# One product for the local scores of two heads: k laid block-diagonally in a fused attention and expert kernel

## The chip, the cores and the metric

The kernel runs on one core of a Trainium2 chip. A core has a matrix engine (TensorE, PE in the profile; its weight loads are listed apart as PEld), VectorE (DVE), ScalarE (ACT), GpSimd (POOL) and a queue that issues transfers (SyncE, SP). Each engine works through its own list of instructions in order and waits on semaphores for the others. [...]

The metric is the device time of one execution in microseconds; lower is better.

## The reference

For 8 batches of 8 heads with 576 positions of 64 numbers, two attentions are added: one over positions averaged by fours (144 of them), repeated four times, and a local one, in which a position sees only the positions less than 4 away.

```python
q_d = q.reshape(B, H, Sd, factor, D).mean(axis=3)          # k_d, v_d alike
out_up = np.repeat(sm_attn(q_d, k_d, v_d), factor, axis=2)
mask = np.abs(pos[:, None] - pos[None, :]) < factor        # factor = 4
scores = scale * np.matmul(q, k.transpose(0, 1, 3, 2))     # scale = 1 / 8
scores = np.where(mask, scores, -1000000000.0)
...                                                        # softmax over the last axis
out_local = np.matmul(attn, v)
return out_up + out_local
```

The sum, with the heads side by side as 4608 tokens of 512 numbers, goes through a mixture of 8 experts: each token is sent to one expert (the largest logit, with a bias by modality), `out = gate * (relu(x @ w1) @ w2)`.

## The kernel before

The attention runs in 32 **steps**, one for two heads; four steps make a batch. The two heads lie above each other in the 128 partitions, head 0 in partitions 0 to 63 and head 1 in 64 to 127. A step n does this:

- `tpq`, `tpk`, `tpt`: TensorE transposes 512 of the 576 positions of q and k (tiles qt and kt, loaded by SP) to PSUM; `tpt`, in every second step, does the remaining 64 of two steps.
- `qT`, `kT_`: ScalarE copies these out of PSUM, to `qT2` and `kT2`. With i = 0 the main 128x512, with i = 1 (every second step) the rest, 128x128. Each has room for two steps, by `n % 2`.
- `mk`, `sc`: the local scores. 576 positions are cut into 24 strips of 24 positions, and a strip sees a window of 32 positions of k. `mk` puts the mask into PSUM with a product, and `sc` adds to it 24 products of 64x24 by 64x32, one for each strip, for one head. Four strips lie in the four quarters of the 128 output partitions. Each 32-bit product shows as two records in the trace. `mk0` and `sc0` do head 0, `mk1` and `sc1` head 1.
- `lm`, `le` (VectorE), `exp` (ScalarE), `z`, `zr` (VectorE), `nl` (GpSimd, a product of tile le with zr), `lt` (VectorE, a transpose), `Pw_` (ScalarE): the softmax of the local scores, and the layout in which `avl` (TensorE) multiplies it with v (tile vw).
- `qe`, `qd`, `d`, `kd`: GpSimd adds q and k by fours, in two sums each; `halves` adds pairs at a distance of two (qe, d), `whole` the rest. `scd`, `dm`, `de`, `nd`, `pdt`, `PdT`, `avd`, `Od` are the averaged attention: scores (TensorE), maximum (VectorE), exponential (ScalarE, tile de), normalization (`nd`, GpSimd, tile de), transposes (`pdt`, TensorE), copies (ScalarE), product with the averaged v (`vp`, `vc` make tile vd), scaling.
- `X`: VectorE adds the two outputs.

Names in the trace are those of tiles: `nl` is GpSimd's instruction on tile le at L391, `nd` that on tile de at L395. The router of a finished batch (`lg` to `st`, `R`, `store`) runs beside the steps of the next: products with the gate, some 20 small VectorE instructions, four or five scatters of table entries by GpSimd (tab), transposes of X (R) and their stores. Behind the attention come the experts: loads of weights, their split into two parts, and products of 512 columns.

The order of work on each engine in the attention is written out by hand: every piece has a time in steps in the table `PHASE` (a piece of step n is issued at n + its time, `kT0` at 0.2050, `sc0` at 0.5591, `zr` at 2.2907 for n two steps earlier), and all pieces are issued in the order of these times. PSUM buffers are shared: tag S (3 buffers) by `mk`/`sc` and `scd`, tag T (3) by the transposes and `vp`, tag A (2) by `avd`, `avl` and the router's products. The functions that the change touches, and their callers:

Of the kernel before, what the change touches and what calls it, by code (L numbers as in the profile page):

```python
# [7 lines left out]
F32 = mybir.dt.float32  # L8
F32R = mybir.dt.float32r
BF16 = mybir.dt.bfloat16  # L10
I32 = mybir.dt.int32
AF = mybir.ActivationFunctionType
ALU = mybir.AluOpType
# [4 lines left out]
B, H, S, D = 8, 8, 576, 64  # L18
# [4 lines left out]
SUB, WIN = 24, 32  # L23
BLK = 4 * SUB
NB = 6
PAD = 3
KT = S - SUB + WIN
QS = 1.0 / 128
NEG = -8.0e9 * QS
# [17 lines left out]
TB, SB = 3, 3  # L47
# [30 lines left out]
class Consts:  # L78
    def __init__(s, tc, pool, psum):
        nc = tc.nc  # L80

        s.ps = psum
        pool.tile([128, 48], F32, name="pad")
        s.dummy = pool.tile([128, 128], BF16, name="dummy")
        nc.vector.memset(s.dummy, 0.0)
        s.busy(nc, 12)
        s.ident = pool.tile([128, 128], F32, name="ident")
        make_identity(nc, s.ident)
        s.identb = pool.tile([128, 128], BF16, name="identb")
        make_identity(nc, s.identb)  # L90

        x = pool.tile([128, 1], F32, name="warm")
        nc.vector.memset(x, 0.0)
        nc.scalar.activation(x, x, AF.Exp)
        m = pool.tile([128, WIN], BF16, name="band")
        nc.gpsimd.memset(m, 0.0)
        for j in range(4):
            t = m[32 * j : 32 * j + 32]
            nc.gpsimd.affine_select(out=t, in_=t, pattern=[[1, WIN]], compare_op=ALU.is_ge, fill=NEG, base=0,
                                    channel_multiplier=-1)  # L100
            nc.gpsimd.affine_select(out=t, in_=t, pattern=[[-1, WIN]], compare_op=ALU.is_ge, fill=NEG, base=6,
                                    channel_multiplier=1)
        s.mask = pool.tile([128, NB, WIN], BF16, name="mask")
        nc.vector.tensor_copy(s.mask, m.unsqueeze(1).broadcast_to([128, NB, WIN]))
        nc.vector.memset(s.mask[0:32, 0, 0:PAD], NEG)
        nc.vector.memset(s.mask[96:128, NB - 1, SUB + PAD : WIN], NEG)

        s.pool = pool.tile([128, 32], F32, name="pool")

# [18 lines left out]
    def load(s, tc, pool, work, rows, mid, bias, w_gate):  # L128
        nc = tc.nc
        s.wg = pool.tile([128, 4, 32], F32, name="wg")  # L130
        nc.vector.memset(s.wg, 0.0)
        for f in range(2):
            for a in range(2):
                nc.sync.dma_start(s.wg[64 * a : 64 * a + 64, 2 * f : 2 * f + 2, 0:NE],
                                  w_gate[256 * f + 128 * a : 256 * f + 128 * a + 128].rearrange("(g d) e -> d g e", g=2))
        s.mi = rows.tile([128, 2 * DM], F32, name="R", bufs=NR)[:36, :256].bitcast(I32)
        nc.sync.dma_start(s.mi, mid.bitcast(I32).rearrange("(t x) -> t x", t=36))
        s.bb = work.tile([128, 2, NE], F32, name="bb")
        nc.sync.dma_start(s.bb, bias.unsqueeze(0).broadcast_to([128, 2, NE]))
# [53 lines left out]
class Attention:  # L193


    def __init__(s, tc, ctx, ectx, C, psum, q, k, v):
        s.tc, s.C, s.ps = tc, C, psum
        nc = s.nc = tc.nc
        s.q, s.k, s.v = q, k, v

        s.ld = ectx.enter_context(tc.tile_pool(name="ald", bufs=2, side="right", reuse_waits="tile"))
        s.wk = ctx.enter_context(tc.tile_pool(name="awk", bufs=2, reuse_waits="tile"))
        s.one = ctx.enter_context(tc.tile_pool(name="aone", bufs=1, reuse_waits="tile"))
        s.QK, s.t = {}, {}
        s.vw = [(s.ld, s.one)[j].tile([128, H * NB, D], F32, name=f"vw{j}", bufs=1) for j in range(2)]

        s.qT2 = s.ld.tile([128, 2, S], F32, name="qT", bufs=1)
        s.kT2 = s.ld.tile([128, 2, KT], F32, name="kT", bufs=1)
        nc.vector.memset(s.kT2[:, :, 0:PAD], 0.0)
        nc.vector.memset(s.kT2[:, :, S + PAD :], 0.0)  # L210
        s.Pw = [s.one.tile([128, 2 * NB, 4, SUB], F32, name=f"Pw{j}") for j in range(NPW)]

        s.De = [s.one.tile([128, 3, 32 * NB], F32, name=f"de{j}") for j in range(3)]
        for j in range(2):
            nc.vector.memset(s.vw[j][0:32, 0], 0.0)
            nc.vector.memset(s.vw[j][96:128, H * NB - 1], 0.0)

        for j in range(3):
            nc.vector.memset(s.De[j], 0.0)
# [49 lines left out]
    def tp(s, n, nm):  # L269

        src = s.QK[n // 2]["qk".index(nm)]
        p = s.t["tp", nm, n] = s.ps.tile([128, 512], F32, name="tp", tag="T", bufs=TB)
        for j in range(4):
            s.nc.tensor.transpose(p[:, 128 * j : 128 * j + 128],
                                  src[:, 5 * (n % 2) + j].rearrange("p a d -> p (a d)"), s.C.ident)
# [7 lines left out]
    def tpt(s, n, i):  # L283

        p = s.t["tp", "t"] = s.ps.tile([128, 2, 128], F32, name="tpt", tag="T", bufs=TB)
        for x in range(2):
            s.nc.tensor.transpose(p[:, x], s.QK[n // 2][x][:, 4].rearrange("p a d -> p (a d)"), s.C.ident)
# [7 lines left out]

    def kT_(s, n, i):
        g = n % 2
        if i:
            t = s.kT2.rearrange("m g t -> m (g t)")[:, PAD + 512 : PAD + 512 + 2 * (KT - 512)]
            s.nc.scalar.copy(t.rearrange("m (g t) -> m g t", g=2)[:, :, :64], s.t["tp", "t"][:, 1].rearrange("m (g t) -> m g t", g=2))  # L300
        else:
            s.nc.scalar.copy(s.kT2[:, g, PAD + 64 * g : PAD + 64 * g + 512], s.t.pop(("tp", "k", n)))

    def halves(s, nm, n, T):

        d2 = s.t[nm, n] = s.ld.tile([128, 144, 2], F32, name=nm, bufs=1)
        T4 = T.rearrange("m (g t) -> m g t", t=4)
        s.nc.gpsimd.tensor_tensor(d2, T4[:, :, 0:2], T4[:, :, 2:4], op=ALU.add)

    def whole(s, nm, n, d2):  # L310
        dd = s.t[nm, n] = s.ld.tile([128, 144], F32, name=nm)
        s.nc.gpsimd.tensor_tensor(dd, d2[:, :, 0], d2[:, :, 1], op=ALU.add)

    def qe(s, n, i):
        s.halves("qe", n, s.qT2[:, n % 2])

    def qd(s, n, i):
        s.whole("qd", n, s.t.pop(("qe", n)))

    def d(s, n, i):  # L320
        s.halves("d", n, s.kT2[:, n % 2, PAD : PAD + S])

    def kd(s, n, i):
        s.whole("kd", n, s.t.pop(("d", n)))

    def mk(s, n, a):
        p = s.t["sc", n, a] = s.ps.tile([128, NB, WIN], F32, name="sc", tag="S", bufs=SB)
        s.nc.tensor.matmul(p, s.C.identb, s.C.mask, start=True, stop=False, skip_group_check=True)

    def sc(s, n, a):  # L330

        p, qT, kT = s.t["sc", n, a], s.qT2[:, n % 2], s.kT2[:, n % 2]
        r = slice(64 * a, 64 * a + 64)
        for i in range(NB):
            for j in range(4):
                q0 = BLK * i + SUB * j
                s.nc.tensor.matmul(p[32 * j : 32 * j + SUB, i, :], qT[r, q0 : q0 + SUB], kT[r, q0 : q0 + WIN],  # L337
                                   start=False, stop=(i == NB - 1), skip_group_check=True,
                                   tile_position=(64 * a, 32 * j))

    def lm(s, n, a):
        if ("lm", n) not in s.t:
# [91 lines left out]
    def avl(s, n, i):  # L434

        b, hp = divmod(n, 4)
        vw, Pw = s.vw[b % 2], s.Pw[n % NPW]
        p = s.t["avl", n, i] = s.ps.tile([128, 3, BLK], F32, name="avl", tag="A", bufs=2)
        for c in range(3):
            for a in range(2):  # L440
                k = 3 * i + c
                s.nc.tensor.matmul(p[64 * a : 64 * a + 64, c], vw[:, NB * (4 * (hp // 2) + hp % 2 + 2 * a) + k, :],
                                   Pw[:, NB * a + k], start=True, stop=True, skip_group_check=True)

    def X(s, n, i, dst):

# [782 lines left out]
```

## Time and profile before

| | |
|---|---|
| median of 3 runs | 709.7 us (709.04 to 718.24) |
| profiled execution | 716.96 us, span of its instructions 715.3 us |
| busy in the span | PE 662.0, PEld 535.7, DVE 379.2, ACT 358.7, POOL 262.9 us |
| TensorE's mean granted clock | 0.974 |
| moved | 107.93 MB, 151 GB/s on the mean |
| local scores (sc) | 7.5 to 257.5 us, 3072 records |

Times in the profile count from the first instruction. A timeline row has the start, the time until the last of its instructions ends, the engine, the line, the operation with its tiles and shapes, and how many instructions it merges; in brackets, idle time of the engine just before it and what ended that. A row of groups has the total busy time, the mean of one in ns, and the idle time before them. A row of stretches has the busy time of PE, PEld, DVE, ACT and POOL in that stretch, each with its number of instructions, then the granted clock, the DMA engines' share and GB/s. Ends of products are modelled, and products overlap, so the distance from one start to the next says more than a duration.

### The profile page before, as it was taken

How to read it: one execution, taken by the hardware profiler on the slowest of the kernel's cores; microseconds unless marked ns; L12 is line 12 of the kernel's file. 1: busy time of each engine (PE TensorE's matmuls, PEld its weight loads, DVE VectorE, ACT ScalarE, POOL GpSimd, SP SyncE). 2: the span in 40 equal slices, each digit the busy share in tenths (PEclk: the TensorE clock that was granted, in tenths of full speed). 3: DMA queues.
4: the chain of work that ended last, by engine and by line, in shares of the span. 5: the costliest groups of instructions: out<-in, count | busy, mean ns of one | idle time of the engine just before them, and what ended most of it. 6: DMA issues, size and time to landing. Idle time of an engine off the chain costs nothing. (4 is left out here: it accounts for less than half of the span.)

```text
span 715.3 us, 19216 instructions
## 1 busy us (share of the span) xinstructions
PE 662.0 (93%) x7467; PEld 535.7 (75%) x7467; DVE 379.2 (53%) x877; ACT 358.7 (50%) x804; POOL 262.9 (37%) x351
## 2 busy tenths in 40 slices
PE   7889999998968798999999999999999999999991
PEld 4677776776746666887888888888888888889790
DVE  3678687787848686836533245333453243525510
ACT  3678777777756574534444234433444234444610
POOL 6756665857647857353030310403103011010200
PEclk9799999999989899999999999999999999999996
DMA  9799799897889757579560744516435154346400
GB/s 178 148 186 173 162 165 181 174 184 130 145 147 214 152 151 186 154 228 294 143 219 21 189 148 116 179 58 190 165 102 156 67 162 148 103 133 186 159 13 29
DMA packets 179439, 107.93 MB, mean 151 GB/s; under 512 B 139309, under 2 KB 157777, under 8 KB 179346
## 3 DMA queue, kind: packets, MB, share of 16 engines
q1 hardware_dynamic: 172274, 87.49, 53.1%
q0 software_dynamic: 7072, 19.18, 8.3%
q8 instruction: 60, 0.98, 0.7%
q14 instruction: 33, 0.27, 0.2%
HBM read 87.39 MB, written 19.51 MB: 149 GB/s over the span
## 5 line engine op out<-in xcount | busy, mean ns | idle before, releaser
L938 POOL DMA_INDIRECT out_dram<-o,tg x37 | 40.9, 1106 | 302.7 <-ACT o L937 245.5
L817 DVE TENSOR_TENSOR wlo<-raw,whi 128x1024 fp32r<-128x1024 f32 x73 | 87.4, 1222 | 84.4 <-ACT whi L811 74.4
L891 DVE SCALAR_TENSOR_TENSOR hl<-l,hh 128x512 fp32r<-128x512 f32 x72 | 49.4, 688 | 101.7 <-ACT hh L890 101.7
L934 PE MATMUL l<-whi,hh 128*128 128x512 f32 x256 | 100.2, 395 | 0.0
L934 PE MATMUL l<-wlo,hh 128*128 128x512 f32 x256 | 99.6, 390 | 0.0
L934 PE MATMUL l<-whi,hl 128*128 128x512 f32 x256 | 99.6, 390 | 0.0
L890 ACT ACTIVATE hh<-l 128x512 fp32r<-128x512 f32 x72 | 42.9, 597 | 110.7 <-PE l L886 109.3
L886 PE MATMUL l<-xh,whi 128*128 128x512 f32 (+1 forms) x256 | 95.0, 374 | 0.4 <-DVE hl L891 0.2
L886 PE MATMUL l<-xh,wlo 128*128 128x512 f32 (+1 forms) x256 | 94.8, 370 | 0.0
L886 PE MATMUL l<-xl,whi 128*128 128x512 f32 (+1 forms) x256 | 94.7, 370 | 0.0
L811 ACT CAST whi<-raw 128x1024 fp32r<-128x1024 f32 x70 | 71.4, 1050 | 28.2 <-DMA raw<-in_moe_w_dram 18.2
L937 ACT ACTIVATE o<-l,tg 128x512 f32<-128x512 f32 x37 | 25.3, 687 | 98.5 <-PE l L934 70.5
L407 ACT COPY Pw<-lt 32x288 f32<-32x288 f32 x128 | 54.6, 426 | 3.2 <-DVE lt L402 1.8
L934 PEld LDWEIGHTS l<-wlo,hh 128*128 128x128 f32 x256 | 48.1, 188 | 10.1
L886 PEld LDWEIGHTS l<-xh,whi 128*128 128x128 f32 x256 | 48.1, 188 | 9.7 <-POOL xg L1063 0.5
L934 PEld LDWEIGHTS l<-whi,hl 128*128 128x128 f32 x256 | 48.1, 188 | 9.5
L934 PEld LDWEIGHTS l<-whi,hh 128*128 128x128 f32 x256 | 48.1, 188 | 9.5
L886 PEld LDWEIGHTS l<-xh,wlo 128*128 128x128 f32 x256 | 48.3, 189 | 8.3
L886 PEld LDWEIGHTS l<-xl,whi 128*128 128x128 f32 x256 | 48.3, 189 | 8.0
L337 PE MATMUL sc<-kT,qT 64*24 64x32 f32 x3072 | 45.5, 195 | 8.1 <-issue 7.4
L391 POOL TENSOR_TENSOR le<-le,zr 128x384 f32<-128x384 f32 x32 | 26.8, 836 | 70.0 <-DVE zr L387 53.5
L337 PEld LDWEIGHTS sc<-kT,qT 64*24 64x24 f32 x3072 | 35.3, 101 | 22.8 <-issue 18.2
(241 smaller groups left out, 1277.9 us busy)
## 6 DMA issues: line engine op xcount, KB each, us to landing
raw<-in_moe_w_dram SPq DMA_DIRECT2D x176, 128.0 KB
raw<-in_moe_w_dram SPq DMA_DIRECT2D x44, 512.0 KB
vw<-in_v_dram SPq DMA_DIRECT2D x53, 192.0 KB
qt<-in_q_dram SPq DMA_DIRECT2D x30, 288.0 KB
kt<-in_k_dram SPq DMA_DIRECT2D x30, 288.0 KB
xs<-R SPq DMA_DIRECT2D x64, 128.0 KB
vw<-in_v_dram SPq DMA_DIRECT2D x15, 96.0 KB
xs<-R SPq DMA_DIRECT2D x12, 64.0 KB
```

The lines of the kernel that those rows point to most:

```text
L337: s.nc.tensor.matmul(p[32 * j : 32 * j + SUB, i, :], qT[r, q0 : q0 + SUB], kT[r, q0 : q0 + WIN], start=False, stop=(i == NB - 1), skip_gro ...
L391: s.nc.gpsimd.tensor_tensor(e, e, z[:, : 2 * NB].unsqueeze(2).broadcast_to([128, 2 * NB, WIN]), op=ALU.mult)
L407: s.nc.scalar.copy(s.Pw[n % NPW][r, :, j, :SUB], s.t["lt", n][r, :, :SUB])
L811: (nc.gpsimd.tensor_copy if turn <= 4 else nc.scalar.copy)(hi, raw)
L817: (nc.gpsimd if turn == 4 else nc.vector).tensor_tensor(lo, raw, hi.bitcast(F32), op=ALU.subtract)
L886: nc.tensor.matmul(p[:, f % n, :], a[:, fs], x[:, k, :N], start=(k == 0 and i == 0), stop=(k == 3 and i == 2))
L890: nc.scalar.activation(hh[:, g, :N], p, AF.Relu)
L891: nc.vector.scalar_tensor_tensor(hl[:, g, :N], p, 0.0, hh[:, g, :N].bitcast(F32), op0=ALU.max, op1=ALU.subtract)
L934: nc.tensor.matmul(p, a[:, f, hs], x[:, f % 2, :], start=(f == 0 and i == 0), stop=(f == 7 and i == 2))
L937: nc.scalar.mul(o, p, T[:, h, 1:2].bitcast(F32))
L938: nc.gpsimd.indirect_dma_start(out=s.out[:, :], out_offset=bass.IndirectOffsetOnAxis(ap=T[:, h, 0:1], axis=0), in_=o, in_offset=None, boun ...
```

## The change

`kT2` becomes `kB`, twice as wide: for each of the two steps that it holds there are two rows of positions, one for each head, and head a's k lies in partitions 64a to 64a + 63 of row a; the rest is cleared once and stays zero. A product over all 128 partitions with a strip of q (both heads above each other) and the same window of both rows gives 64 columns: the scores of head 0 and of head 1 beside each other. `sc` now goes by halves of the positions (x = 0, 1) with both heads, 12 products of 128x24 by 128x64 in each call, where it went by heads with 24. The copies of k out of PSUM split by head: of the main part ScalarE copies 64x512 and VectorE the other 64x512; of the rest ScalarE makes four copies of 64x64. The half sums of k (`d`) become two instructions of 64 partitions. The mask needs two forms, since the first and the last strip now lie in different calls, and `avl` reads the weights in the new order of blocks.

```diff
-        nc.vector.memset(s.mask[0:32, 0, 0:PAD], NEG)
-        nc.vector.memset(s.mask[96:128, NB - 1, SUB + PAD : WIN], NEG)
+        nc.vector.memset(s.mask[0:32, 0:2, 0:PAD], NEG)
+        s.band = m
...
-        s.kT2 = s.ld.tile([128, 2, KT], F32, name="kT", bufs=1)
-        nc.vector.memset(s.kT2[:, :, 0:PAD], 0.0)
-        nc.vector.memset(s.kT2[:, :, S + PAD :], 0.0)
+        s.kB = s.ld.tile([128, 2, 2, KT], F32, name="kT", bufs=1)
+        nc.vector.memset(s.kB, 0.0)
+        s.mask = s.one.tile([128, NB, WIN], BF16, name="mask")
+        nc.vector.tensor_copy(s.mask, C.band.unsqueeze(1).broadcast_to([128, NB, WIN]))
+        nc.vector.memset(s.mask[96:128, NB - 2 :, SUB + PAD : WIN], NEG)
...
     def kT_(s, n, i):
         g = n % 2
-        if i:
-            t = s.kT2.rearrange("m g t -> m (g t)")[:, PAD + 512 : PAD + 512 + 2 * (KT - 512)]
-            s.nc.scalar.copy(t.rearrange("m (g t) -> m g t", g=2)[:, :, :64], s.t["tp", "t"][:, 1].rearrange("m (g t) -> m g t", g=2))
-        else:
-            s.nc.scalar.copy(s.kT2[:, g, PAD + 64 * g : PAD + 64 * g + 512], s.t.pop(("tp", "k", n)))
+        p = s.t["tp", "t"][:, 1] if i else s.t.pop(("tp", "k", n))
+        for a in range(2):
+            r = slice(64 * a, 64 * a + 64)
+            if i:
+                t = s.kB[r].rearrange("m g a t -> m g (a t)")[:, :, KT * a + PAD : KT * a + PAD + 512 + 64]
+                s.nc.scalar.copy(t[:, 0, 512:], p[r, :64])
+                s.nc.scalar.copy(t[:, 1, :64], p[r, 64:])
+            else:
+                (s.nc.vector.tensor_copy if a else s.nc.scalar.copy)(s.kB[r, g, a, PAD + 64 * g : PAD + 64 * g + 512], p[r])

     def halves(s, nm, n, T):
 
         d2 = s.t[nm, n] = s.ld.tile([128, 144, 2], F32, name=nm, bufs=1)
-        T4 = T.rearrange("m (g t) -> m g t", t=4)
-        s.nc.gpsimd.tensor_tensor(d2, T4[:, :, 0:2], T4[:, :, 2:4], op=ALU.add)
+        for t, x in T:
+            T4 = x.rearrange("m (g t) -> m g t", t=4)
+            s.nc.gpsimd.tensor_tensor(d2[t], T4[:, :, 0:2], T4[:, :, 2:4], op=ALU.add)
...
     def d(s, n, i):
-        s.halves("d", n, s.kT2[:, n % 2, PAD : PAD + S])
+        r = [slice(64 * a, 64 * a + 64) for a in range(2)]
+        s.halves("d", n, [(r[a], s.kB[r[a], n % 2, a, PAD : PAD + S]) for a in range(2)])
...
-    def sc(s, n, a):
-
-        p, qT, kT = s.t["sc", n, a], s.qT2[:, n % 2], s.kT2[:, n % 2]
-        r = slice(64 * a, 64 * a + 64)
-        for i in range(NB):
+    def mk(s, n, x):
+        p = s.t["sc", n, x] = s.ps.tile([128, NB, WIN], F32, name="sc", tag="S", bufs=SB)
+        s.nc.tensor.matmul(p, s.C.identb, s.mask if x else s.C.mask, start=True, stop=False, skip_group_check=True)
+
+    def sc(s, n, x):
+
+        p, qT, kB = s.t["sc", n, x], s.qT2[:, n % 2], s.kB[:, n % 2]
+        for i in range(NB // 2):
             for j in range(4):
-                q0 = BLK * i + SUB * j
-                s.nc.tensor.matmul(p[32 * j : 32 * j + SUB, i, :], qT[r, q0 : q0 + SUB], kT[r, q0 : q0 + WIN],
-                                   start=False, stop=(i == NB - 1), skip_group_check=True,
-                                   tile_position=(64 * a, 32 * j))
+                q0 = BLK * (NB // 2 * x + i) + SUB * j
+                s.nc.tensor.matmul(p[32 * j : 32 * j + SUB, 2 * i : 2 * i + 2, :], qT[:, q0 : q0 + SUB],
+                                   kB[:, :, q0 : q0 + WIN], start=False, stop=(i == NB // 2 - 1),
+                                   skip_group_check=True, tile_position=(0, 32 * j))
...
-                                   Pw[:, NB * a + k], start=True, stop=True, skip_group_check=True)
+                                   Pw[:, 2 * k + a], start=True, stop=True, skip_group_check=True)
```

More of the change, by code (lines that the diff above doesn't have):

```diff
@@ L314, in qe @@
     def qe(s, n, i):
-        s.halves("qe", n, s.qT2[:, n % 2])
+        s.halves("qe", n, [(slice(0, 128), s.qT2[:, n % 2])])
     def qd(s, n, i):
@@ L320, in d @@
     def d(s, n, i):
-        s.halves("d", n, s.kT2[:, n % 2, PAD : PAD + S])
+        r = [slice(64 * a, 64 * a + 64) for a in range(2)]
+        s.halves("d", n, [(r[a], s.kB[r[a], n % 2, a, PAD : PAD + S]) for a in range(2)])
     def kd(s, n, i):
         s.whole("kd", n, s.t.pop(("d", n)))
-    def mk(s, n, a):
-        p = s.t["sc", n, a] = s.ps.tile([128, NB, WIN], F32, name="sc", tag="S", bufs=SB)
-        s.nc.tensor.matmul(p, s.C.identb, s.C.mask, start=True, stop=False, skip_group_check=True)
-    def sc(s, n, a):
-        p, qT, kT = s.t["sc", n, a], s.qT2[:, n % 2], s.kT2[:, n % 2]
-        r = slice(64 * a, 64 * a + 64)
-        for i in range(NB):
+    def mk(s, n, x):
[4 more added lines that the diff above has]
+        for i in range(NB // 2):
             for j in range(4):
-                q0 = BLK * i + SUB * j
-                s.nc.tensor.matmul(p[32 * j : 32 * j + SUB, i, :], qT[r, q0 : q0 + SUB], kT[r, q0 : q0 + WIN],
-                                   start=False, stop=(i == NB - 1), skip_group_check=True,
-                                   tile_position=(64 * a, 32 * j))
+                q0 = BLK * (NB // 2 * x + i) + SUB * j
+                s.nc.tensor.matmul(p[32 * j : 32 * j + SUB, 2 * i : 2 * i + 2, :], qT[:, q0 : q0 + SUB],
+                                   kB[:, :, q0 : q0 + WIN], start=False, stop=(i == NB // 2 - 1),
+                                   skip_group_check=True, tile_position=(0, 32 * j))
     def lm(s, n, a):
```

## The prediction

> **What bounds the kernel now.** I began with the page's busy times and the waits, then took the stage that the change touches apart with the stretch table and the timeline of TensorE. The first rows give the whole, the extent of the local scores, and one stretch behind them.
>
> ```profile
> PE 662.0 (93%) x7467; PEld 535.7 (75%) x7467; DVE 379.2 (53%) x877; ACT 358.7 (50%) x804; POOL 262.9 (37%) x351
> L337 PE MATMUL sc<-kT,qT x3072: 186/190/247, 7.5 to 257.5; 64*24 64x32 f32 x192
> 400.00:450.00 50.00, 50.00 (x236) 41.64 (x235) 18.15 (x21) 19.09 (x27) 10.26 (x10) 1.00 0.47 137
> ```
>
> TensorE carries the span: 662.0 of 715.3 us, and all 50.00 of 50 us behind the attention. The local scores lie from 7.5 to 257.5 us. What the change moves must happen there; the part behind has none of its instructions and shifts as a whole. So the question is what sets the pace of the 32 steps. I cut one batch (four steps, numbers 12 to 15) at the first transpose of q in each. After the length of a step come the busy times of PE, PEld, DVE, ACT and POOL.
>
> ```profile
> 91.13:98.30 7.17, 7.00 (x174) 5.55 (x171) 6.89 (x25) 5.63 (x18) 3.51 (x5) 1.00 0.81 186
> 98.30:105.80 7.50, 6.36 (x159) 5.09 (x158) 5.18 (x15) 5.46 (x17) 6.88 (x10) 1.00 1.29 149
> 105.80:113.78 7.98, 7.24 (x173) 5.60 (x172) 4.41 (x12) 5.66 (x18) 6.14 (x10) 1.00 0.86 171
> 113.78:122.34 8.56, 7.83 (x184) 5.69 (x182) 6.83 (x23) 6.51 (x21) 4.14 (x7) 1.00 0.95 185
> ```
>
> No single engine sets all four. In step 12 VectorE is busy 6.89 of 7.17 us, with the router's work of the batch before on it, and TensorE 7.00. In step 13 GpSimd is busy 6.88 of 7.50. Steps 14 and 15 have room on DVE and POOL. TensorE's marks (the start of the transposes pdt of each step) show who holds it:
>
> ```profile
> 97.52 0.86 PE L413 MATMUL pdt<-ident,de 128*96 128x128 f32 x6
> ...
> 105.02 0.86 PE L413 MATMUL pdt<-ident,de 128*96 128x128 f32 x6 [0.28 <-POOL de L395]
> ...
> 107.06 0.58 PE L337 MATMUL sc<-kT,qT 64*24 64x32 f32 x43
> 107.93 0.25 PE L337 MATMUL sc<-kT,qT 64*24 64x32 f32 x3 [0.28 <-issue]
> 108.64 0.24 PE L337 MATMUL sc<-kT,qT 64*24 64x32 f32 x2 [0.46 <-issue]
> 108.80 1.06 PE L262 MATMUL vp<-vw,pool 128*32 128x256 f32 x12
> ...
> 113.00 0.86 PE L413 MATMUL pdt<-ident,de 128*96 128x128 f32 x6
> ...
> 121.27 0.86 PE L413 MATMUL pdt<-ident,de 128*96 128x128 f32 x6
> ...
> 127.86 0.60 PE L337 MATMUL sc<-kT,qT 64*24 64x32 f32 x48
> 128.40 0.86 PE L413 MATMUL pdt<-ident,de 128*96 128x128 f32 x6
> ```
>
> At 105.02 TensorE waits for GpSimd's product de. A call of sc without a stall is the last pair: from 127.86 to 128.40 is 0.54 us for 48 records (24 products, two records each), 11.2 ns apart. The call at 107.06 is cut by two waits that nothing in the profile releases and ends at 108.80: 1.74 us, 1.20 more. Of this the timeline shows 0.28 + 0.46 = 0.74 as idle time. Over the middle of the stage (60 to 250 us) the view of waits has:
>
> ```profile
> PE sc L337 <- issue: 7.4, 16, 0.8
> q8 instruction: 60, 0.98, 0.7%
> ```
>
> 16 such waits, 7.4 us. At the ratio above (1.20 for 0.74) I estimate their cost at 12.0 us. I take them for instructions that come late: queue q8 moved 0.98 MB, which for 7467 products and as many weight loads is 66 bytes each, and sc, at a product and a load in 11.2 ns, uses them up fastest. [...]
>
> **What it removes.** *Products.* There are two calls of sc a step, 64 in all, as before, but each has 12 products of 64 columns in place of 24 of 32: 24 records for 48. The trace has no such product; lg is nearest in kind, full depth in four column groups:
>
> ```profile
> 54.55 1.07 PE L489 MATMUL lg<-X,wg 128*32 128x256 f32 x16
> 55.55 0.60 PE L337 MATMUL sc<-kT,qT 64*24 64x32 f32 x48
> ...
> 84.27 1.28 PE L489 MATMUL lg<-X,wg 128*32 128x320 f32 x16
> 85.49 0.60 PE L337 MATMUL sc<-kT,qT 64*24 64x32 f32 x48
> ```
>
> From 256 to 320 columns the 16 records go from 1.00 to 1.22 us, so a column costs (1.22 - 1.00) / 16 / 64 = 0.21 ns a record, and 256 of them leave 62.5 - 54 = 8.5 ns of each record fixed. Lower end: records cost 11.2 ns whatever their width, 24 x 11.2 = 0.27 us a call. Upper end: lg's fixed part, 24 x (8.5 + 13.4) = 0.53 us, nothing gained. I take sc's own 11.2 plus 32 more columns, 24 x 17.9 = 0.43 us, in the middle: 0.11 us a call, 0.22 a step, 7.0 us over 32 steps of TensorE time. *Stalls.* sc issues half as many instructions over four fifths of the time. Between none and all of the 12.0 us may go; I take two thirds, 8.0 us, and 0.80 of the 1.20 us in step 14. mk and avl read other places of the same size: nothing.
>
> **What it adds.** The rows for copies and half sums:
>
> ```profile
> L267 DVE COPY vd<-vp 96x512 f32<-96x512 f32 x12 | 8.1, 675 | 0.0
> L302 ACT COPY kT<-tp 128x512 f32<-128x512 f32 x23 | 13.4, 584 | 0.6 <-PE tp L274 0.5
> L300 ACT COPY kT<-tpt 128x128 f32<-128x128 f32 x12 | 3.1, 262 | 0.0
> L308 POOL TENSOR_TENSOR d<-kT 128x288 f32<-128x288 f32 x23 | 15.4, 669 | 1.4 <-ACT kT L300 1.3
> 1.52 0.29 POOL masks.py:199 TENSOR_SCALAR_AFFINE_SELECT identb<-identb 128x128 bf16<-128x128 bf16 x1
> 1.76 0.20 POOL L99 TENSOR_SCALAR_AFFINE_SELECT band<-band 32x32 bf16<-32x32 bf16 x1
> ```
>
> - VectorE: a copy of 64x512 out of PSUM in every step. The copy of 96x512 took 675 ns: +0.68 us a step.
> - ScalarE: its copy keeps 512 columns, so 584 ns as before. The copy of 128 columns (262 ns) becomes four of 64. By the line through these two rows (0.84 ns a column) one is 208 ns, between 0.2 and 0.26: +0.57 us in two steps. ScalarE's idle time hides it (busy 5.63 of 7.17 us in step 12): nothing, and 0.29 us a step if that room goes.
> - GpSimd: the sum d of 128x288 becomes two of 64x288. If its time went with all elements, both would cost the 669 ns of one; if with columns, twice. The select over 128x128 has 16 times the elements of the one over 32x32 and takes 0.29 for 0.20 us, so columns: +0.67 us a step, with 0 as the other end.
> - At the start VectorE clears 128x2336:
>
> ```profile
> 1.81 1.75 DVE L219 MEMSET de<- 128x576 f32 x3 [0.16 <-issue]
> ...
> 8.16 0.36 DVE L344 TENSOR_REDUCE lm<-sc 128x6 f32<-128x192 f32 x1 [3.83 <-PE sc L337]
> ...
> 15.72 1.08 PE L274 MATMUL tp<-ident,kt 128*128 128x128 f32 x4 [3.47 <-DMA kt<-in_k_dram]
> ```
>
> 576 columns took 1.75 / 3 = 0.58 us, so 2.4 us, and 0.2 for a second mask. VectorE is idle for 3.83 us ahead of its first maximum, and behind it TensorE waits 3.47 us for k's load. Nothing; 2.6 us without both.
>
> The new copy waits for the transposes of k, and VectorE works in order. Behind it stand zr, then lm, le and lt of the step; for zr GpSimd's le waits:
>
> ```profile
> 106.23 0.60 PE L274 MATMUL tp<-ident,kt 128*128 128x128 f32 x4
> 106.33 0.25 DVE L387 RECIPROCAL zr<-zr 128x15 f32<-128x15 f32 x1
> ```
>
> Here zr, at 106.33, would stand until the transposes end (106.83) and the copy is through, 107.5. GpSimd is late enough in this step for that to cost nothing; in step 12 it isn't. No DMA is moved, and none is added: SP's queue is as before.
>
> **The sum over a batch.** The chain through step 12 and 13:
>
> ```profile
> 94.14 0.25 DVE L387 RECIPROCAL zr<-zr 128x15 f32<-128x15 f32 x1
> 94.54 0.83 POOL L391 TENSOR_TENSOR le<-le,zr 128x384 f32<-128x384 f32 x1 [6.94 <-ACT qT L292]
> 96.54 0.92 POOL L395 TENSOR_TENSOR de<-de,zr 128x432 f32<-128x432 f32 x1
> 104.04 0.93 POOL L395 TENSOR_TENSOR de<-de,zr 128x432 f32<-128x432 f32 x1
> 109.18 0.92 POOL L395 TENSOR_TENSOR de<-de,zr 128x432 f32<-128x432 f32 x1
> ```
>
> - Step 12: VectorE has no room, so zr and with it GpSimd's le (94.54) and de (96.54) come 0.68 later; pdt at 97.52 starts as de ends: +0.68.
> - Step 13: GpSimd, idle for 0.62 of 7.50 us, has no pause to give up on its way to de at 104.04, and one more half sum in it: +0.68 + 0.67 = +1.35 at the mark of 105.02. TensorE's own gain here, its stalls too, is lost in this wait.
> - Step 14: TensorE's pace, -0.22 - 0.80: +0.33 at the mark of 113.00. GpSimd's de, at 109.18 + 0.68 + 2 x 0.67 + 0.92 = 112.1, is in time.
> - Step 15: -0.22: +0.11 at 121.27. VectorE, 6.83 + 0.68 of 8.56, has room.
>
> So what TensorE gains in two steps is what the helpers lose in the other two. The router works beside seven batches: +0.8 us. The eight steps ahead of it have room on all helpers: 8 x -0.22 = -1.8. Together -1.0 us, nothing. The profiled execution took 716.96 us, 7.3 over the median of 709.7; some of the stalls may belong to profiling. A difference of -1.0 gives 709.
>
> **Rivals.**
> - *TensorE sets the pace everywhere*, helpers' additions lie in gaps. For it: in the stretch table TensorE is busy at least 6.36 in every step. Against it: the wait at 105.02. -7.0 - 8.0 = -15.0: 695 us.
> - *Records, not columns, cost*: a call falls to 0.27 us, 64 x 0.27 = -17.3, and with the stalls -25.3: 684 us. For it: the 11.2 ns a record is more than 32 columns' 6.7; against it lg's slope. [...]
> - *The change doesn't reach TensorE*: the call stays at 0.53 us and the late instructions stall the products beside it instead. The helpers' +1.35 a batch stays: 7 x 1.35 = 9.5, 719 us.
> - *GpSimd and VectorE become the bound* (slower): the half sum and the copy hold a third step as well, +0.68 + 2 x 0.67 = 2.0 us a batch, 14.1 us, 724 us. It decides once GpSimd's de of step 14 (112.1) is later than TensorE's mark there, that is if GpSimd loses another 1.3 us. Against it: POOL is 3.51 of 7.17 in step 12.
>
> **Chances.** Forecast 0.55 (704 to 714), TensorE alone 0.12, records 0.03, not reached 0.18, helpers bound 0.12. 2% is 14.2 us, about what a measurement can tell from no change: under 695.5 lie half of TensorE alone and the records, 0.09; over 723.9 half of the helpers and a little of the fourth, 0.08; 0.83 between. The range of 697 to 721 leaves out most of the 695 and the 724 case, about 0.2.
>
> **What would show it.** In the profile after: calls of sc at 0.43 us; sc's "issue" waits in the stage a third of 7.4 us; VectorE's kT copy at 0.6 to 0.7 us; d in 64 records near 0.67; pdt waiting for de in every second step of a batch, longer than 0.28; the last sc near 257. Wrong if pdt does not wait and the last sc comes before 245 (TensorE alone), or if it comes after 265.

## The result, and the profile after

The changed kernel took 754.0 us (median of 4 runs, 751.97 to 756.9) beside 709.64 us for the kernel before (4 runs, 709.04 to 718.24). The ratio is 1.0619, 95% interval 1.057 to 1.0668: slower by some 44 us, where 709 was predicted and 697 to 721 given as the range. The profiled execution took 756.9 us, 39.9 more than that of before, which was itself 7 us above its median.

Of the kernel after, the page's busy times, then the local scores' extent, and the same stretch behind the attention as was shown of before:

```profile
PE 668.4 (89%) x5931; PEld 536.6 (71%) x5931; DVE 408.4 (54%) x909; ACT 364.2 (48%) x852; POOL 283.0 (37%) x383
```

```profile
L344 PE MATMUL sc<-kT,qT x1536: 216/219/314, 8.9 to 292.5; 128*24 128x64 f32 x192
```

```profile
400.00:450.00 50.00, 50.00 (x232) 41.44 (x231) 17.61 (x20) 18.05 (x25) 11.13 (x12) 1.00 0.47 144
```

Half of sc's products are gone (5931 matmuls in all, for 7467), and from 400 us on TensorE is as full as before. The last product of the local scores comes at 292.5 us instead of 257.5: 35 of the 39.9 us are lost up to there. The rest lies where the experts begin: from 350 to 400 us TensorE is busy for 43.5 us, where it was for 50.0, and its products wait there for VectorE and ScalarE (6.5 us); what holds those up was not followed. In the attention TensorE now stands. These are waits of the kernel after in the first 300 us (total, times, longest, all in us):

```profile
POOL d L315 <- DMA tab<-ig,si: 30.8, 13, 4.1
...
DVE kT L308 <- ACT kT L308: 30.2, 21, 3.2
...
PE scd L371 <- POOL kd L319: 24.5, 11, 4.4
PE pdt L420 <- POOL de L402: 12.1, 12, 2.8
PE pr L561 <- DVE X L460: 8.8, 4, 2.2
PE pr L561 <- DVE late L460: 4.9, 3, 1.8
```

and the rows of the kernel before that answer to the last three (it had none of the first three):

```profile
PE pdt L413 <- POOL de L395: 5.2, 6, 3.8
...
PE pr L554 <- DVE late L453: 1.5, 1, 1.5
...
PE pr L554 <- DVE X L453: 0.5, 1, 0.5
```

Two waits are new on the helpers. GpSimd's half sum d waits for the router's scatters into its table, and VectorE's copy of k waits for ScalarE's. Three of TensorE's have grown: scd for kd (24.5 us, from nothing), pdt for de (12.1 from 5.2), the router's products pr for X and late (13.7 from 2.0). The experiments will show that the first goes for the most part with the wait for the scatters and the last with the copy's; pdt's does not go with either. The timeline of the kernel after shows both at work in one step, put together from the four engines' rows in order of engine:

```profile
68.32 1.18 POOL L606 DMA_INDIRECT tab<-ig,si  x1 [0.17 <-issue]
...
71.53 0.66 POOL L315 TENSOR_TENSOR d<-kT 64x288 f32<-64x288 f32 x1
74.08 0.66 POOL L315 TENSOR_TENSOR d<-kT 64x288 f32<-64x288 f32 x1 [1.89 <-DMA tab<-ig,si]
...
76.09 0.42 POOL L319 TENSOR_TENSOR kd<-d 128x144 f32<-128x144 f32 x1
...
72.13 0.60 PE L276 MATMUL tp<-ident,kt 128*128 128x128 f32 x4
...
76.57 0.95 PE L371 MATMUL scd<-kd,qd 64*64 64x144 f32 x12 [2.65 <-POOL kd L319]
...
73.11 0.58 ACT L308 COPY kT<-tp 64x512 f32<-64x512 f32 x1
...
72.14 0.54 DVE L388 TENSOR_REDUCE z<-le 128x12 f32<-128x384 f32 x1
73.72 0.69 DVE L308 COPY kT<-tp 64x512 f32<-64x512 f32 x1 [1.03 <-ACT kT L308]
74.45 0.17 DVE L393 TENSOR_SCALAR zr<-z 128x15 f32<-128x15 f32 x1
```

The first half sum (71.53, partitions 0 to 63) runs as soon as what stands ahead of it is done. The second (74.08, partitions 64 to 127) is next in GpSimd's order, and yet GpSimd stands for 1.89 us: it is released by the scatter that began at 68.32, 5.8 us earlier. So kd is done at 76.51, and scd on TensorE, idle for 2.65 us, starts at 76.57. On VectorE the copy starts at 73.72, 0.03 us after ScalarE's copy of the other half has ended (73.11 + 0.58), though the transposes of k were through at 72.73. z had ended at 72.68, and zr stands behind the copy until 74.45.

The pieces themselves came out near the prediction. One call of sc to the next product in the timeline, and the groups of sc, d and the copy (busy us, mean ns, and behind the bar the idle time ahead of them):

```profile
288.31 0.54 PE L344 MATMUL sc<-kT,qT 128*24 128x64 f32 x24
288.77 0.86 PE L420 MATMUL pdt<-ident,de 128*96 128x128 f32 x6
```

```profile
L344 PE MATMUL sc<-kT,qT 128*24 128x64 f32 x1536 | 37.7, 235 | 1.8 <-DVE kT L308 1.3 <-issue 0.5
...
L315 POOL TENSOR_TENSOR d<-kT 64x288 f32<-64x288 f32 x64 | 42.8, 668 | 38.5 <-DMA tab<-ig,si 30.8
...
L308 DVE COPY kT<-tp 64x512 f32<-64x512 f32 x32 | 22.2, 695 | 31.5 <-ACT kT L308 30.2 <-ACT qT L296 0.9
```

This call, with pdt behind it, takes 0.46 us (0.54 before, 0.43 predicted), d 668 ns a half (0.67), the copy 695 ns (0.68). The idle time ahead of d and of the copy, behind the bar, is what the prediction had not priced.

### The profile page after: what moved, and what is told of

The parts are those of the page before. It is cut to its first block, busy times and chain, and to the rows that moved or that the text cites. A ratio compares the mean times of both kernels' runs of the same rounds, so it can differ in the third digit from the quotient of the medians.

```text
span 755.2 us, 16289 instructions
## 1 busy us (share of the span) xinstructions
PE 668.4 (89%) x5931; PEld 536.6 (71%) x5931; DVE 408.4 (54%) x909; ACT 364.2 (48%) x852; POOL 283.0 (37%) x383
## 5 line engine op out<-in xcount | busy, mean ns | idle before, releaser
L818 ACT CAST whi<-raw 128x1024 fp32r<-128x1024 f32 x70 | 71.4, 1050 | 35.7 <-DMA raw<-in_moe_w_dram 22.3
L315 POOL TENSOR_TENSOR d<-kT 64x288 f32<-64x288 f32 x64 | 42.8, 668 | 38.5 <-DMA tab<-ig,si 30.8
L371 PE MATMUL scd<-kd,qd 64*64 64x144 f32 x384 | 33.5, 311 | 25.0 <-POOL kd L319 24.5
L845 POOL DMA_INDIRECT xg<-xs,tg x37 | 38.6, 1043 | 31.3 <-DMA tg<-tab 8.5
```

Of the source, the lines that this page charges most:

```text
L315: s.nc.gpsimd.tensor_tensor(d2[t], T4[:, :, 0:2], T4[:, :, 2:4], op=ALU.add)
L371: s.nc.tensor.matmul(p[r, c, :], qd[r, 40 * c : 40 * c + 64], kd[r, :], start=True, stop=True, skip_group_check=True)
L818: (nc.gpsimd.tensor_copy if turn <= 4 else nc.scalar.copy)(hi, raw)
L845: nc.gpsimd.indirect_dma_start(out=R[:, h, :], out_offset=None, in_=s.xs[:n, :], in_offset=bass.IndirectOffsetOnAxis(ap=T[:, h, 0:1], axis ...
```

## The experiments

Three theories were tested. **T1**, the scatter wait: the half sum over partitions 64 to 127 waits for the router's scatters, and kd, scd and de come late. **T2**, the copy wait: VectorE's copy waits for ScalarE's out of the same tile, and VectorE's later work queues behind it. **T3**, the work: the added busy time on VectorE and GpSimd costs, and the waits only show it. The expectations down to e8 count 16 steps where there are 32, so the work that they name for T3 is half of what it is; where that matters it is said below.

All times beside the kernel before, on the same chip (ratio with 95% interval):

| kernel | median us | ratio |
|---|---|---|
| changed, both copies on ScalarE (e1) | 743.86 | 1.0446 (1.0392 to 1.0499) |
| changed, half sums over 128 partitions (e2) | 723.52 | 1.0163 (1.0112 to 1.0214) |
| both of these (e3) | 709.03 | 0.9996 (0.9962 to 1.0029) |
| before, half sum split by partitions (e4) | 737.49 | 1.0339 (1.0274 to 1.0404) |
| before, copy of k split over two engines (e5) | 726.12 | 1.0232 (1.0174 to 1.0290) |
| the product's form alone (e7) | 704.18 | 0.9923 (0.9887 to 0.9958) |
| whole computation, no half sum from partition 64 (e8) | 712.42 | 1.0036 (1.0002 to 1.0071) |
| e3 and an addition on VectorE, 64x600 (e10) | 723.58 | 1.0188 (1.0127 to 1.0250) |
| e3 and the copy's wait without its work (e11) | 718.65 | 1.0100 (1.0062 to 1.0139) |
| e3 and an addition on VectorE, 64x480 (e13) | 720.80 | 1.0139 (1.0084 to 1.0193) |
| e3 and a maximum on VectorE, 64x528 (e14) | 718.79 | 1.0085 (1.0053 to 1.0116) |
| whole computation, dense copy of k for d (e9) | 711.62 | 1.0011 (0.9982 to 1.0041) |

The kernel before had medians of 708.6 to 713.8 us over these sets, so differences are taken between ratios, times 709.6; they are uncertain by some 4 us.

### Both copies of k on ScalarE (e1)

```diff
-                (s.nc.vector.tensor_copy if a else s.nc.scalar.copy)(s.kB[r, g, a, ...], p[r])
+                s.nc.scalar.copy(s.kB[r, g, a, ...], p[r])
```

> The changed kernel with both 64x512 copies of k of a step on ScalarE, so VectorE has neither the copy nor its wait. Theory T1 (the half sum over partitions 64 to 127 waits for the router's table scatters, and kd, scd and de come late from it): nearly all of the loss stays, 745 to 755 us, the waits of scd for kd stay near 24 us. T2 (VectorE's copy waits for ScalarE's copy of the same tile and VectorE's queue is held up behind it): pr's waits for X and late (13.7 us) go, about 738 to 742 us. T3 (no wait matters, the added busy time of VectorE and GpSimd does): VectorE loses 16 x 0.70 us, ScalarE gains 16 x 0.58, about 740 us, with scd's waits shorter too.

Measured 743.86 us, 12 us less than the changed kernel by the ratios, between T1's number and T2's. The wait for kd stays, even longer, and those of pr are small:

```profile
PE scd L371 <- POOL kd L319: 29.9, 11, 4.3
...
PE pr L561 <- DVE late L460: 2.3, 3, 1.3
...
PE pr L561 <- DVE X L460: 1.9, 4, 0.6
```

T1's large part is untouched; taking the copy off VectorE was worth 12 us, by its wait or its work.

### Half sums over all partitions (e2), and both edits (e3)

```diff
-        s.halves("d", n, [(r[a], s.kB[r[a], n % 2, a, PAD : PAD + S]) for a in range(2)])
+        w = slice(0, 128)
+        s.halves("d", n, [(w, s.kB[w, n % 2, a, PAD : PAD + S]) for a in range(2)])
```

> The changed kernel with the half sums of k as two sums over all 128 partitions each (the same two instructions of 64-by-288 size a partition on GpSimd; the second writes over the first, so the averaged k of head 0 is left out). T1: without the wait for the scatters the 30.8 us of GpSimd's waits go, scd's wait for kd falls from 24.5 to under 6 us, and the time falls by 25 to 35 us, to 720 to 730 us. T2: the time stays within 5 us of 754. T3 (added work): GpSimd's work is the same, 754 us.

> Both edits: the copies of k on ScalarE alone, and the half sums over 128 partitions (the averaged k of head 0 left out). T1 and T2 together: 705 to 715 us, back at the kernel before, since the two waits make the whole loss. T1 alone: as with the half sums over 128 partitions alone, 720 to 730 us. T3: GpSimd's added work of 16 x 0.67 us is still there, 735 to 745 us.

e2 has the same two sums of 288 columns on GpSimd and no wait for the table in its list. Its waits:

```profile
DVE kT L308 <- ACT kT L308: 29.7, 21, 2.0
...
PE pr L562 <- DVE X L461: 8.8, 4, 2.2
PE scd L372 <- POOL kd L319: 6.6, 7, 1.1
PE pr L562 <- DVE late L461: 6.1, 3, 2.6
```

723.52 us: 32 us less than the changed kernel, with the work as it was. T1 held to its number and T3 falls for GpSimd. VectorE's wait and pr's remain; with the copies on ScalarE too (e3) they go (pr: 3.9 us in all), and the time is that of the kernel before, 0.9996. One wait does not go, and so is no part of the loss that the two edits bring back:

```profile
PE pdt L421 <- POOL de L403: 12.8, 13, 2.3
```

By the ratios the scatter wait is 4.5% with VectorE's copy or without it (1.0619 - 1.0163, 1.0446 - 0.9996), the copy 1.7% either way: 32 and 12 us, together the whole 44.

### The half sum split in the kernel before (e4)

```diff
-        s.nc.gpsimd.tensor_tensor(d2, T4[:, :, 0:2], T4[:, :, 2:4], op=ALU.add)
+        for r in [slice(0, 128)] if nm == "qe" else [slice(0, 64), slice(64, 128)]:
+            s.nc.gpsimd.tensor_tensor(d2[r], T4[r, :, 0:2], T4[r, :, 2:4], op=ALU.add)
```

> The kernel before with its one half sum of k in two, partitions 0 to 63 and 64 to 127, and nothing else changed. T1: the second sum waits for the table scatters as in the changed kernel, some 30 us of waits in GpSimd, and the time rises by 20 to 35 us, to 730 to 745 us. T2: nothing but 16 x 0.67 us of work, 710 to 714 us. T3: the half of the added work that lies on GpSimd, 715 to 722 us.

737.49 us, T1's number, in a kernel that has neither the new product nor the new copy. By the ratio it is 24 us, the second sum's work among them:

```profile
POOL d L309 <- DMA tab<-ig,si: 38.9, 18, 4.4
...
PE scd L365 <- POOL kd L313: 26.7, 12, 4.9
```

In the compiled program 19 of the 32 sums over partitions 64 to 127 carry a wait for the scatters issued so far, and none of those over 0 to 63 or over all 128. So it is a semaphore wait that the program asks for, and no run shows whether the chip needs it. The wait goes with the place, not with the order: put first, the sum over 64 to 127 has it still in the compiled program. Why the program asks for it is open; no run took it away from this instruction itself.

### The copy split in the kernel before (e5)

```diff
-            s.nc.scalar.copy(s.kT2[:, g, ...], s.t.pop(("tp", "k", n)))
+            p = s.t.pop(("tp", "k", n))
+            s.nc.scalar.copy(s.kT2[:64, g, ...], p[:64])
+            s.nc.vector.tensor_copy(s.kT2[64:, g, ...], p[64:])
```

> The kernel before with its copy of k in two: 64x512 on ScalarE and 64x512 on VectorE out of the same tile, into the same dense kT. T2 (the wait for ScalarE's copy and what queues behind it on VectorE): waits of VectorE's copy for ScalarE's of some 30 us, and a time of 717 to 725 us. T1 (the scatter wait alone): VectorE's copy is beside the path, 707 to 711 us. T3 (added busy time): VectorE gains 16 x 0.70 us, 712 to 720 us, with no wait for ScalarE's copy that matters.

726.12 us, 16 more than before and 1 above T2's range, with the wait that T2 names, in the list of waits and in the timeline:

```profile
DVE kT L304 <- ACT kT L303: 24.4, 18, 2.9
```

```profile
72.49 0.69 DVE L304 COPY kT<-tp 64x512 f32<-64x512 f32 x1 [0.95 <-ACT kT L303]
...
71.89 0.57 ACT L303 COPY kT<-tp 64x512 f32<-64x512 f32 x1
```

Again VectorE's copy starts as ScalarE's ends (72.46). With T3's step count put right (22 us of work) the time alone would not tell T2 from T3 here; the runs below take work and wait apart. The two copies read different partitions of one tile and write different partitions of another. The traces show that they are ordered all the same, for 24.4 us in 18 waits here and 30.2 us in 21 after the change. Here too it is the program that asks: in its compiled form each of VectorE's 32 copies carries a wait for ScalarE. Whether the chip needs that order no run shows.

### The product's form alone (e7)

```diff
-                (s.nc.vector.tensor_copy if a else s.nc.scalar.copy)(s.kB[r, g, a, ...], p[r])
+            elif a == 0:
+                s.nc.scalar.copy(s.kB[r, g, a, ...], p[r])
...
-        s.halves("d", n, [(r[a], s.kB[r[a], n % 2, a, PAD : PAD + S]) for a in range(2)])
+        w = slice(0, 128)
+        s.halves("d", n, [(w, s.kB[w, n % 2, 0, PAD : PAD + S])])
```

> The products of the changed kernel with the helpers' work of the kernel before: the copy of head 1's k and its half sum are left out (one 64x512 copy on ScalarE, one half sum over 128 partitions), so head 1's local scores lack k. What the new form of the product is worth alone: by the trace 48 calls' worth of stalls and 64 x 0.07 us. If the products set the end, 692 to 700 us; if the helpers' chains do (T1 and T2 both hold and nothing else is on the path), 702 to 710 us.

704.18 us, 0.9923, what was expected if the helpers' chains set the end: the new product alone, with the helpers loaded as before, is worth 5.5 us (3.0 to 8.0). TensorE's calls are shorter, and the waits for "issue" (7.4 us before) are gone from sc's row of products. What it gained there it loses again in large part in waiting for the helpers, 22.6 us where pdt waited 5.2 before, one wait of 9.1 us among them:

```profile
L345 PE MATMUL sc<-kT,qT 128*24 128x64 f32 x1536 | 34.7, 223 | 0.4 <-ACT kT L308 0.4
```

```profile
PE pdt L421 <- POOL de L403: 22.6, 13, 9.1
```

### The whole computation without a half sum from partition 64 (e8)

```diff
 # beside both copies on ScalarE
+        for a in range(2):
+            s.halves(f"d{a}", n, [(slice(0, 128), s.kB[:, n % 2, a, PAD : PAD + S])])
...
+        for a in range(2):
+            s.whole(f"kd{a}", n, s.t.pop((f"d{a}", n)))
...
-                s.nc.tensor.matmul(p[r, c, :], qd[r, 40 * c : 40 * c + 64], kd[r, :], ...)
+                s.nc.tensor.matmul(p[r, c, :], qd[r, 40 * c : 40 * c + 64], kd[a][r, :], ...)
```

> The whole computation: the changed kernel with both copies of k on ScalarE, and two half sums and two whole sums of k over all 128 partitions, of which the scores of the averaged rows take head 0's half from the one and head 1's from the other. No half sum over partitions 64 to 127 alone. T1 and T2: about as the kernel with the averaged k of head 0 left out, 705 to 715 us, with GpSimd's second whole sum (16 x 0.35 us) at most 5 us of it. T3: GpSimd's added work counts, 720 us or more.

712.42 us, 1.0036. Nothing is left out here, GpSimd has 32 whole sums more than in e3, and 41 of the 44 us are back. It is not faster than the kernel before.

### Is it VectorE's wait or its work? (e10, e13, e14, e11)

e10 and e13 put work without a wait where the copy stood in e3:

```diff
+                if a:
+                    s.nc.vector.tensor_tensor(s.w[1][r], s.w[0][r], s.w[0][r], op=ALU.add)   # 600 columns, then 480
```

> The changed kernel with the copies of k on ScalarE and the half sums over 128 partitions (the averaged k of head 0 left out, measured at 709.0 us), and on VectorE, at the place where its copy of k stood, an addition of 64x600 f32 from a constant tile into one that nobody reads: the copy's work of about 0.7 us without its wait for ScalarE. T2: the wait was what cost, so 707 to 713 us. T3: VectorE's work was what cost, so 720 to 726 us, as with the copy on VectorE (723.5).

> The work without the wait, now of the copy's own length: as the run with the 64x600 addition on VectorE (which took 854 ns each, 27.3 us in all), with 64x480, some 0.69 us each and 22 us in all. T3: in proportion to the busy time, 709 + 14.5 x 22/27 = 721 us (718 to 724). T2: had the longer work only come out at the same time by its length, the right length costs little, 709 to 714 us.

Measured 1.0188 and 1.0139, T3's numbers and not T2's. But the groups of e10 show that it was not VectorE's time alone:

```profile
L312 DVE TENSOR_TENSOR w<-w 64x600 f32<-64x600 f32 x32 | 27.3, 854 | 0.9
...
L319 POOL TENSOR_TENSOR d<-kT 128x288 f32<-128x288 f32 x64 | 47.6, 743 | 2.5
```

GpSimd's half sums take 743 ns here and 726 in e13 (beside additions of 740 ns), where they took 666 in e3: 4 to 5 us more on GpSimd in all. Beside VectorE's additions, which have two inputs, a half sum took 60 to 77 ns longer on the mean; by what means is not shown. So both runs were confounded, and e14 took an operation with one input:

```diff
+                if a:
+                    s.nc.vector.tensor_reduce(s.w[1][r], s.w[0][r], op=ALU.max, axis=AX.X)   # 528 columns to 1
```

> The work without the wait, of another kind: the addition on VectorE read two tiles of the chip's SBUF and GpSimd's half sums beside it grew from 666 to 726 and 743 ns, so that its 11 to 15 us may be GpSimd's. Here VectorE does a maximum over 64x528 of one constant tile instead (one input, one number a partition out, some 0.7 us, 22 us in all), in the kernel with the copies of k on ScalarE and the half sums over 128 partitions (the averaged k of head 0 left out, 709.0 us). T3, VectorE's time counts of itself: GpSimd's half sums stay near 666 ns and the time is 716 to 722 us. T2, only the wait counts (measured without the work at 718.7): 707 to 712 us.

```profile
L312 DVE TENSOR_REDUCE w<-w 64x1 f32<-64x528 f32 x32 | 22.4, 699 | 0.9
...
L319 POOL TENSOR_TENSOR d<-kT 128x288 f32<-128x288 f32 x64 | 42.6, 666 | 2.5
```

1.0085, with GpSimd's sums at 666 ns: 22.4 us of work on VectorE cost 6 us, by the ratio the low end of T3's range. And the wait without the work:

```diff
+                o, w = PAD + 64 * g, 480 if a else 512
+                s.nc.scalar.copy(s.kB[r, g, a, o : o + w], p[r, :w])
+                if a:
+                    s.nc.vector.tensor_copy(s.kB[r, g, a, o + w : o + 512], p[r, w:])
```

> The wait without the work: the kernel with the copies of k on ScalarE and the half sums over 128 partitions (the averaged k of head 0 left out, 709.0 us), in which VectorE copies the last 32 columns of head 1 out of the same tile (64x32, some 0.1 us) and ScalarE the 480 ahead of them. VectorE's copy waits for ScalarE's two and its queue stands behind it. (There are 32 steps: 32 copies of 0.69 us are 22 us, where the earlier expectations counted 16.) T2, the wait is what costs: 720 to 726 us, pr's waits for X and late near 15 us. T3, VectorE's occupied time by the copy's work is what costs: 708 to 714 us.

```profile
L311 DVE COPY kT<-tp 64x32 f32<-64x32 f32 x32 | 6.2, 195 | 38.5 <-ACT kT L309 38.2
```

```profile
PE pr L565 <- DVE X L464: 6.3, 4, 1.6
...
PE pr L565 <- DVE late L464: 4.9, 3, 2.6
```

1.0100: 38.2 us of waiting with 6.2 us of copying cost 7 us, between T3's number and T2's, and pr waits 11.2 us where T2 said 15. Against e3 the work alone is 0.9%, the wait alone 1.0%, and both at once, as the change has them (e2), 1.7%. Neither T2 nor T3 holds alone: work and wait cost about alike, and together no more than their sum. A reading that fits is that VectorE is held at this place, whether it works or stands, and that a part of it falls into gaps that it had anyway; no run tests it, and the costs of 6, 7 and 12 us for some 22, 44 and 52 us held are not in proportion. e3 still had such gaps, of VectorE waiting for GpSimd's le and for sc (the first two rows below); in e11 the one has shrunk to the row shown last and the other is all but gone:

```profile
DVE lt L410 <- POOL le L399: 17.9, 15, 2.8
DVE lm L352 <- PE sc L345: 11.9, 16, 2.6
```

```profile
DVE lt L413 <- POOL le L402: 3.3, 8, 0.9
```

### A dense copy of k for the half sum (e9)

```diff
 # beside both copies on ScalarE
+            s.nc.scalar.copy(s.kT2[:, g, 64 * g : 64 * g + 512], p)
...
+        s.halves("d", n, [(slice(0, 128), s.kT2[:, n % 2])])
```

> The whole computation with the new product, and GpSimd as in the kernel before: ScalarE makes a dense copy of k (128x512) beside the two 64x512 ones into the block-diagonal tile, and the one half sum over 128 partitions reads the dense copy. VectorE has no copy. ScalarE gains 32 x 1.15 us against the kernel before. T1 and T2: neither wait is left, and ScalarE is at 0.75 of its time in the attention, so 703 to 710 us. T3: ScalarE's added work of 37 us counts as VectorE's did (some 0.6 of it), 722 to 730 us.

711.62 us, 1.0011: the whole computation at the speed of the kernel before, with GpSimd and VectorE as there and ScalarE loaded more. By the ratio it is at the upper end of what T1 and T2 expected, and T3's number is far off: ScalarE had room for most of it. But the 5.5 us of the product's form are used up: TensorE now waits for ScalarE here,

```profile
PE avl L453 <- ACT Pw L418: 7.9, 9, 1.1
PE tp L277 <- ACT PdT L431: 5.3, 11, 0.6
```

so no version was found that is faster than the kernel before. e7 shows what there is to gain, under 1%.

## Why the prediction was wrong

By the runs the 44 us are: -5.5 the product's form (e7), +5 the second half sum's and the second copy's work (e7 to e3), +32 the scatter wait, +12 VectorE's copy (e3 to e2), of which, apart, the work makes 6 and the wait 7. Each of these numbers is uncertain by some 4 us.

- **The half sums.** "+0.67 us a step" was the duration, and it was right (668 ns). The step that failed is that nothing else was asked of the second instruction. The prediction bounded how long it runs and not what it may wait for; the list of waits of the kernel before has no such wait, because no sum of GpSimd started at partition 64 there. It added 30.8 us in 13 waits, 2.4 us each, and cost 32. That SP's queue and the DMAs stayed as they were was true, and the scatters of GpSimd's own queue were not looked at.
- **The copy.** "The new copy waits for the transposes of k" named the wrong releaser. It waits for ScalarE's copy of the other half (30.2 us in 21 waits). The consequence was named: zr, lm, le and lt stand behind it. It was priced at +0.68 in one step of four; in the timeline above zr could have followed z at 72.7 and came at 74.45, 1.8 us later.
- **The sum over a batch.** e14 has about what was summed: the new product, the work on all helpers, and neither wait (besides, ScalarE makes both copies of k in it). It comes to 1.0085, +6 us (4 to 8), for -1.0 predicted. That is a miss of 7 us, inside the range; the other 38 come with the waits. What was foretold for pdt came true, it waits for de 12 times, and cost little: e3 has that wait at the time of the kernel before.
- **The products.** This term came out within 1 us. A call with pdt behind it takes 0.46 us for 0.54; one with vp behind it, 16 of the 64, takes 0.35 (72.15 to 72.50 us in e7) for 0.61 (62.35 to 62.96 before). 48 x 0.08 + 16 x 0.25 = 8 us of TensorE time, for 7.0 predicted. A call of 0.27, as records alone would have it, is refuted. The form alone was to give 15 us where TensorE sets the pace, and gave 5.5 (e7): in e7 it doesn't set the pace, and pdt's wait for de is 17 us longer than before.
- **The stalls.** They went as said and further (sc's waits for "issue", 7.4 us, are down to 0.5). Whether they bring the 8.0 us is open, for no run shows that term: e7's 5.5 us are less than the calls alone, since the waits for de take up what is gained, and no run takes the two apart. That these waits are for instructions that come late was the prediction's own estimate; the traces name no releaser for them. In e4, which has the old product, these waits fell too, to 0.2 us, while TensorE stood elsewhere (26.7 us for kd). The ratio of 1.20 us lost for 0.74 idle came from one call.

- **What hid at nothing.** ScalarE's four copies took 201 and 209 ns on the mean (208 predicted), and in e9 ScalarE does nearly 40 us more than before, at a cost of some 6 us (e7 to e9). The clearing at the start took 2.0 us for 2.4.
- **The rivals.** "GpSimd and VectorE become the bound" (0.12, 724 us) is the one that came. Its point of decision, GpSimd losing another 1.3 us in a step (by its own marks 113.00 + 0.33 - 112.1 = 1.2), was passed by the wait of 2.4 us. Its price was too small by the same omission: it counted the helpers' work in three steps and no wait. "Wrong if the last sc comes after 265" was met, at 292.

## What to carry to other kernels

A part that was split into two instructions on the same engine, or over two engines, brought waits here beside its durations: for each new instruction ask what it must wait for that the whole one did not. Two sources of such waits were measured in the changed kernel: an engine's own transfers under way (GpSimd's scatters, 30.8 us in 13 waits), and another engine that reads the same tile (ScalarE, 30.2 us in 21). A helper that has no wait of its own in the old profile may have one in the new, and its length can count like work: 38.2 us of waiting with 6.2 of copying cost 7 us (e11), 22.4 us of work alone 6 (e14). A wait that stops TensorE can cost more than its length: from the changed kernel to e2 scd's wait for kd fell by 18 us and the time by 32 (below).

## What was not expected of the hardware

- In this program a sum on GpSimd over partitions 64 to 127 waits for scatters that GpSimd has issued (38.9 us in 18 waits, 4.4 us at the longest, in e4); the same sum over all 128 partitions, or over 0 to 63, does not. The wait is the program's, and whether the chip needs it is open. The sum takes the same time over 64 partitions as over 128, 668 and 666 ns for 288 columns.
- An addition on VectorE beside GpSimd's sums made these slower by a tenth (666 to 726 and 743 ns); beside a maximum with one input they took 666 ns.
- The mean granted clock of TensorE was 0.954 in the profiled run of the changed kernel, for 0.974 before and 0.986 in e3; in e1 and e4, with long waits of TensorE too, it was 0.965. Most of the difference lies in the attention. The first 300 us of the changed kernel, then of e3:

```profile
0.00:300.00 300.00, 238.09 (x3821) 179.38 (x3821) 217.55 (x623) 189.86 (x607) 190.46 (x299) 0.90 0.77 148
```

```profile
0.00:300.00 300.00, 259.41 (x4085) 197.79 (x4086) 225.64 (x681) 226.56 (x675) 213.53 (x319) 0.99 0.88 170
```

In the changed kernel the clock falls to half for 3.4 to 6.8 us at a time, twelve times between 60 and 290 us, and each time TensorE was busy for less than half of the 3.4 us ahead (1.63 us at the most). After one more such stretch, from 177.36 with 1.62 us busy, the clock stayed at 1.00. One place where it fell, the stretch ahead of it and the stretch at half clock:

```profile
245.55:248.96 3.41, 1.10 (x15) 0.81 (x14) 2.83 (x5) 1.73 (x8) 3.15 (x5) 1.00 0.89 236
...
248.97:255.79 6.82, 5.48 (x58) 3.68 (x58) 6.40 (x23) 3.32 (x8) 3.91 (x6) 0.50 0.38 99
```

Four transposes that take 0.60 us at 72.13 take 1.06 at 251.60. Over the same 5931 products the idle times ahead of TensorE's groups add up to 71.4 us in the changed kernel and 43.9 in e3. Of the 50 us between these two profiled executions, then, some 27 are time in which TensorE stands, and 23 are products that take longer, at half clock for the most part it seems. So the waits can cost more than their length: from the changed kernel to e2 scd's wait for kd falls by 18 us, and the time by 32. That the clock falls because TensorE stood is what the order suggests; no run tested it.
